# Attention output transposed and in column halves, scores in row halves, gate logits in strips of four tiles

## The chip, the cores and the metric

The kernel runs on one core of a Trainium2 chip. The metric is the device time of one execution in microseconds. TensorE (PE) multiplies matrices, VectorE (DVE), ScalarE (ACT) and GpSimd (POOL) work element by element, SyncE (SP) issues most DMAs. Every engine takes its instructions strictly in the order of the program and waits at an instruction until what it needs is there. TensorE works on operands in SBUF and writes into PSUM, which ACT and VectorE empty. Its clock is granted at one of two levels, 1.2 and 2.4 GHz.

## What is computed

Three stages follow one another. The attention is a recurrence with a decay per element, for 4 batches of 8 heads, 768 steps and head size 48:

```python
state = np.zeros((B, H, D, D), dtype=np.float32)
for t in range(S):
    state = alpha[:, :, t, :, None] * state + np.einsum('bhd,bhe->bhde', k[:, :, t], v[:, :, t])
    y[:, :, t] = np.einsum('bhd,bhde->bhe', q[:, :, t], state)
```

Its output, 3072 rows of 384, goes through a mixture of eight experts: `logits = x @ w_gate + modality_bias[modality_id]`, one expert per row (the argmax), `gate_w * (relu(x @ w1[e]) @ w2[e])` with the softmax weight of that expert. A dense layer follows, `relu(x @ w_in)**2 @ w_out`. All of it is in float32.

## The kernel before

The 3072 rows are 24 tiles of 128 (`NTILE`), six to a batch. The program is written out by hand in the order in which each engine is to run it; no scheduler changes it. The loop over the tiles (lines 732 to 776) does this in iteration n:

- TensorE: `kv_mm(n)`, the tile's contribution to the state; `qk_mm(n + 1)`, the scores of the next tile; `k_T(n + 1)`, its keys transposed (kp); `gate_T(n - 1)`, the output rows of the tile before, transposed for the gate; `y_mm(n)`; `gate_L(n - 1)`, its logits.
- VectorE: the state's update (st, sd) in `kv_mm`, then `prep(n + 3)`: the running products of the decay (acum), the reverse ones (rs), and queries and keys scaled by them (qt, kt). Behind these, weight conversions for the dense layer (`conv_v`, in iterations up to 15), the gate (`gate_a` and what follows), and from iteration 20 the splitting of expert weights (`pop`).
- ACT empties PSUM: scores (pa), kp (kT), the gate's transposes (xt), the output (xb); it builds two block-diagonal operands by copies, qbd of the queries (`q_bd`) and sbd of the state (`s_bd`); and it scales output rows by their gate weight (`scale`).
- GpSimd masks the scores (pm) and does a part of the conversions.

Heads stand in pairs: qt, kt and the state hold head 2p in partitions 0 to 47 and head 2p+1 in 64 to 111 (`RP` = 112). Before, a pair's scores are one matmul over 112 partitions with the block-diagonal qbd (256 columns), and y has the tile's rows in its partitions. `y_mm` first adds the part of the state (L514, from the second tile of a batch on), then that of the tile (L517). A float32 matmul leaves two records of the multiplication and two of the weight load in the trace (a transpose leaves one of each).

The tiles are gated in groups of 8, 8, 5 and 3 (`GROUPS`). Once a group's last tile is there, `gate_a` on VectorE finds the expert; in the next iteration `gate_b` on TensorE counts rows per expert and stands ahead of `y_mm`. After group 1 (tiles 8 to 15) the fullest expert is chosen, its weights are loaded, and rows for it are gathered (iteration 21), so that its matmuls (`mm1(0, f)`) start right behind the loop. `scale` and `store` write the scaled rows to DRAM (xs), from where the experts gather them. `ps_x` is a PSUM pool with one bank (tag "x"), which gate transposes, the row lists and the experts' transposes share. `open_moe` behind the loop lets GpSimd fill x2T with zeros, in the space that the attention leaves. Groups' functions and the loop, as the change touches them:

## Time and profile before

| | |
|---|---|
| runs | 870.28, 874.29, 2774.08 us (median 874.29) |
| profiled execution | 871.33 us, span 869.5 us |
| TensorE busy | 819.9 us (94%), weight loads 733.8 us (84%) |
| VectorE, ACT, GpSimd busy | 508.3 us (58%), 369.4 us (42%), 198.9 us (23%) |
| mean granted TensorE clock | 0.951 |

The attention takes the first quarter of the span: y of the last tile begins at 206.8 us. The experts' and the dense layer's matmuls fill the rest. A busy share is an average over the span; which engine sets the pace of a stage is read from the stage. Names such as `y<-vv,pm` say what an instruction writes and from what; L517 is a line of the kernel before.

### The profile page before, as it was taken

What the parts mean: (1) busy time and instruction counts of PE and PEld (TensorE: products, weight loads), DVE (VectorE), ACT (ScalarE), POOL (GpSimd) and SP (SyncE); (2) the same over time, 40 slices, a digit from 0 to 9 for tenths busy, and PEclk for the clock granted to TensorE, in tenths of its full rate; (3) what the DMA queues carried; (4) which work ended last, traced back from release to release, by engine and by line L of the source; (5) the groups of instructions that cost most, each with busy time, mean ns of one, the idle gap of its engine ahead of it and who ended that gap; (6) DMA issues with size and microseconds to landing.
All of it is one profiled execution on the core that took longest, in us unless ns stands there. A gap on an engine that the chain in (4) does not pass through costs nothing.

```text
span 869.5 us, 12270 instructions
## 1 busy us (share of the span) xinstructions
PE 819.9 (94%) x4704; PEld 733.8 (84%) x4704; DVE 508.3 (58%) x823; ACT 369.4 (42%) x663; POOL 198.9 (23%) x179
## 2 busy tenths in 40 slices
PE   6998789799889999999979999999999999999995
PEld 5988779699888778787868999999999999999985
DVE  7999999886747365464576444454454334334340
ACT  3655476296244344444445333333233234234331
POOL 6355355234123242331230001001001001000101
PEclk8888689699999999999989999999999999999998
DMA  9765475462445667558565002102100000000001
GB/s 238 188 195 178 145 249 163 135 196 96 137 118 185 179 127 203 113 185 157 86 217 145 21 1 83 51 1 77 58 1 28 11 0 23 15 1 19 19 0 41
DMA packets 42542, 88.75 MB, mean 102 GB/s; under 512 B 11134, under 2 KB 26522, under 8 KB 42474
## 3 DMA queue, kind: packets, MB, share of 16 engines
q1 hardware_dynamic: 39274, 78.04, 33.0%
q0 software_dynamic: 3200, 9.83, 3.5%
q8 instruction: 39, 0.64, 0.3%
q14 instruction: 29, 0.24, 0.1%
HBM read 72.10 MB, written 15.76 MB: 101 GB/s over the span
## 4 chain that ended last, share of the span: by engine, by line
PE 72%; DVE 18%; DMA 5%; ACT 2%; issue 2%; POOL 0%; SPq 0%; POOLq 0%; DVEq 0%; ACTq 0%
PE h L620 8%; PE h L621 8%; PE acc L621 8%; PE acc L619 8%; PE acc L620 8%; PE h L619 8%; PE oo L620 3%; PE hps L619 3%; PE hps L620 3%; PE oo L621 3%; PE oo L619 3%; PE hps L621 3%; DVE acum L435 3%; DVE rs L439 2%; PE y L517 2%
## 5 line engine op out<-in xcount | busy, mean ns | idle before, releaser
L966 DVE TENSOR_TENSOR r<-r 128x512 f32<-128x512 f32 x96 | 66.6, 693 | 149.5 <-ACT r L965 149.4
L621 PE MATMUL acc<-w2h,hl 128*128 128x384 f32 x376 | 126.8, 337 | 0.0
L965 ACT ACTIVATE r<-h 128x512 f32<-128x512 f32 x96 | 57.4, 598 | 162.9 <-PE h L621 161.0
L619 PE MATMUL acc<-w2h,hh 128*128 128x384 f32 x376 | 126.6, 337 | 0.0
L620 PE MATMUL acc<-w2l,hh 128*128 128x384 f32 x376 | 126.3, 336 | 0.0
L621 PE MATMUL h<-xh,w1l 128*128 128x512 f32 x288 | 113.9, 395 | 0.0
L620 PE MATMUL h<-xl,w1h 128*128 128x512 f32 x288 | 113.6, 395 | 0.0
L619 PE MATMUL h<-xh,w1h 128*128 128x512 f32 x288 | 112.2, 390 | 0.0
L989 POOL DMA_INDIRECT out_dram<-ob,pidx x24 | 24.3, 1011 | 383.9 <-ACT ob L987 346.5
L530 DVE TENSOR_TENSOR hl<-r,hh 128x512 fp32r<-128x512 f32 x94 | 65.1, 693 | 64.5 <-PE acc L621 39.8
L529 ACT CAST hh<-r 128x512 fp32r<-128x512 f32 x94 | 58.3, 621 | 75.5 <-DVE r L966 75.5
L620 PE MATMUL oo<-hl,w2h 128*128 128x512 f32 (+1 forms) x192 | 68.8, 358 | 6.4 <-DVE hl L881 6.4
L619 PEld LDWEIGHTS acc<-w2h,hh 128*128 128x128 f32 x376 | 70.7, 188 | 4.1
L620 PEld LDWEIGHTS acc<-w2l,hh 128*128 128x128 f32 x376 | 70.6, 188 | 4.0
L621 PEld LDWEIGHTS acc<-w2h,hl 128*128 128x128 f32 x376 | 70.5, 188 | 0.0
L881 DVE SCALAR_TENSOR_TENSOR hl<-hps,hh 128x512 fp32r<-128x512 f32 (+1 forms) x48 | 30.9, 644 | 67.5 <-ACT hh L880 67.5
L619 PE MATMUL hps<-xh,w1h 128*128 128x512 f32 (+1 forms) x192 | 67.8, 353 | 2.6 <-DVE hl L645 2.6
L619 PE MATMUL oo<-hh,w2h 128*128 128x512 f32 (+1 forms) x192 | 70.1, 365 | 0.0
L621 PE MATMUL oo<-hh,w2l 128*128 128x512 f32 (+1 forms) x192 | 68.5, 357 | 0.0
L465 POOL TENSOR_SCALAR_AFFINE_SELECT pm<-pa 128x512 f32<-128x512 f32 x48 | 49.4, 1039 | 82.8 <-ACT pa L463 82.5
L620 PE MATMUL hps<-xl,w1h 128*128 128x512 f32 (+1 forms) x192 | 67.2, 350 | 0.1
L621 PE MATMUL hps<-xh,w1l 128*128 128x512 f32 (+1 forms) x192 | 67.1, 349 | 0.0
(223 smaller groups left out, 1571.7 us busy)
## 6 DMA issues: line engine op xcount, KB each, us to landing
qk<-qka_dram SPq DMA_DIRECT2D x23, 675.5 KB, 5.3
raw<-w_dram SPq DMA_DIRECT2D x21, 512.0 KB, 7.9
raw<-w_dram SPq DMA_DIRECT2D x28, 384.0 KB, 3.6
raw<-w_in_dram SPq DMA_DIRECT2D x12, 512.0 KB, 6.2
cvr<-w_out_dram SPq DMA_DIRECT2D x12, 512.0 KB, 9.8
vv<-v_dram SPq DMA_DIRECT2D x24, 192.0 KB, 5.3
xs<-xb SPq DMA_DIRECT2D x24, 192.0 KB, 2.3
alr<-alpha_dram SPq DMA_DIRECT2D x9, 512.0 KB, 3.6
```

Of the source, the lines that this page charges most:

```text
L435: V.tensor_tensor_scan(acum.rearrange("p a c -> p (a c)"), al, one0.rearrange("p a c -> p (a c)"), 0.0, op0=ALU.mult, op1=ALU.max)
L439: V.tensor_tensor_scan(rs.rearrange("p a c -> p (a c)")[:, ::-1], al[:, ::-1], rz.rearrange("p a c -> p (a c)")[:, ::-1], 0.0, op0=ALU.mul ...
L465: G.affine_select(out=pmt, in_=pa, pattern=[[0, 4], [1, C]], compare_op=ALU.is_ge, fill=0.0, base=0, channel_multiplier=-1)
L529: A.copy(hi, raw)
L530: V.tensor_sub(lo, raw, hi)
L619: PE.matmul(o, ah, bh, start=start, stop=False)
L620: PE.matmul(o, ah, bl, start=False, stop=False)
L621: PE.matmul(o, al, bh, start=False, stop=stop)
L881: V.scalar_tensor_tensor(hl, o, 0.0, hh, op0=ALU.max, op1=ALU.subtract)
L965: A.activation(r, o, AF.Relu)
L966: V.tensor_mul(r, r, r)
L989: G.indirect_dma_start(out=out, out_offset=bass.IndirectOffsetOnAxis(ap=pidx[:, n:n + 1], axis=0), in_=ob, in_offset=None)
```

## The change

Scores: no block-diagonal queries any more. Each head's scores are a matmul of its own over its 48 partitions, heads of partitions 0 to 47 into one PSUM bank and those of 64 to 111 into another, in turns. Output: y is computed transposed, [112 partitions, 4 pairs, 128 rows]; the state's operand sbd becomes a 112 x 112 block matrix that is now the stationary one, and the tile's part is one matmul per head with v as stationary operand, into partitions 0 to 63 or 64 to 111 (the 16 columns over 48 are other data that nothing reads). Gate: the transposed output needs no transpose for the logits; `gate_lg` computes those of up to four tiles in four strips of 32 partitions, ACT copies them, and one transpose turns them back. `scale` now transposes the tile's output back to rows (four transposes into ps_x) and ACT scales while it empties PSUM, in two instructions; `store` follows at once. Up to three tiles an iteration are scaled, at three places (`ts`), where before three or four were scaled at its end.

```diff
@@ -116,21 +116,22 @@
...
-    NQ, NR = 2, 2
+    NR = 2
     one0 = at1.tile([RP, NP, CA], F32, name="one0")
     G.memset(one0, AMIN)
     G.memset(one0[:, :, :1], 1.0)
-    qbd = [at1.tile([RP, NP, 2, C], F32, name=f"qbd{i}") for i in range(NQ)]
-    sbd = [at1.tile([RP, NP, 2, D], F32, name=f"sbd{i}") for i in range(2)]
+    sbd = [at1.tile([RP, NP, RP], F32, name=f"sbd{i}") for i in range(2)]
     raz = [at1.tile([RP, NP, CA], F32, name=f"raz{i}") for i in range(NR)]
     for i in range(WARM):
         wps = ps_a.tile([128, 4, C], F32, tag="sp", name="warm", bufs=2)
         PE.matmul(wps.rearrange("p a c -> p (a c)")[:, :256], one0[:, 0, :128], one0.rearrange("p a c -> p (a c)")[:, :256], start=True, stop=True)
-    for t in raz + qbd + sbd:
+    for t in raz + sbd:
         G.memset(t, 0.0)
 
-    wg_sb = gc.tile([128, KD, NE], F32, name="wg_sb")
-    SY.dma_start(wg_sb, wg.rearrange("(k p) e -> p k e", p=128))
+    wg_sb = gc.tile([RP, NP, 32], F32, name="wg_sb")
+    G.memset(wg_sb, 0.0)
+    for j in range(2):
+        SY.dma_start(wg_sb[64 * j:64 * j + D, :, :NE], wg.rearrange("(p j d) e -> j d p e", j=2, d=D)[j])
...
@@ -196,27 +197,26 @@
 
     gst = {}
 
-    def gate_T(x):
-        xt_ps = ps_x.tile([128, 512], F32, tag="x", name="xt_ps")
-        for k in range(KD):
-            PE.transpose(xt_ps[:, k * 128:(k + 1) * 128], x[:, k * 128:(k + 1) * 128], ident)
-        xt = gt.tile([128, DM], F32, tag="xt", name="xt")
-        A.copy(xt, xt_ps[:, :DM])
-        return xt
-
-    def gate_L(g, i, xt):
-        if i == 0:
-            gst[g] = dict(lg=ps_g.tile([128, GM, NE], F32, tag="lg", name="lg"))
-        lg = gst[g]["lg"]
-        for k in range(KD):
-            PE.matmul(lg[:, i, :], xt[:, k * 128:(k + 1) * 128], wg_sb[:, k, :], start=(k == 0), stop=(k == KD - 1))
+    def gate_lg(g, i0, i1):
+        t0 = GROUPS[g][0]
+        lt = ps_g.tile([128, 128], F32, tag="lt", name="lt")
+        for p in range(NP):
+            for i in range(i0, i1):
+                q = slice(32 * (i - i0), 32 * (i - i0 + 1))
+                PE.matmul(lt[q, :], wg_sb[:, p, :], yts[t0 + i][:, p, :], start=(p == 0), stop=(p == NP - 1))
+        n = 32 * (i1 - i0)
+        ls = gt.tile([128, 128], F32, tag="ls", name="ls")
+        A.copy(ls[:n], lt[:n])
+        if i0 == 0:
+            gst[g] = dict(lg=ps_g.tile([128, GM, 32], F32, tag="rk", name="lg"))
+        PE.transpose(gst[g]["lg"][:, i0:i1, :].rearrange("p t e -> p (t e)"), ls[:n], ident[:n, :n])
 
...
-        V.tensor_add(L, lg[:, :T, :], lbias[:, t0:t0 + T, :])
+        V.tensor_add(L, lg[:, :T, :NE], lbias[:, t0:t0 + T, :])
...
@@ -268,10 +268,18 @@
 
     def scale(t):
         g, i = tile_group[t]
-        A.activation(xts[t], xts[t], AF.Copy, scale=gst[g]["gw"][:, i:i + 1])
+        xp_ = ps_x.tile([128, 512], F32, tag="x", name="xtr")
+        yt = yts.pop(t)
+        for p in range(NP):
+            PE.transpose(xp_[:, p * RP:(p + 1) * RP], yt[:, p, :], ident[:RP, :RP])
+        x = gt.tile([128, DM], F32, tag="xb", name="xb", bufs=3)
+        xv = xp_[:, :NP * RP].rearrange("s (p r) -> s p r", r=RP)
+        for j in range(2):
+            A.activation(x.rearrange("s (p j d) -> s j p d", j=2, d=D)[:, j], xv[:, :, 64 * j:64 * j + D], AF.Copy, scale=gst[g]["gw"][:, i:i + 1])
+        xts[t] = x
 
     def store(t):
-        SY.dma_start(xs[t * 128:(t + 1) * 128, :], xts[t])
+        SY.dma_start(xs[t * 128:(t + 1) * 128, :], xts.pop(t))
 
     def gate_bt(t):
         g, i = tile_group[t]
@@ -444,21 +452,17 @@
         ae = acum[:, :, C:C + 1]
         return dict(ae=ae, qt=qt, kt=kt)
 
-    def q_bd(n):
-        qb, qt = qbd[n % NQ], preps[n]["qt"]
-        A.copy(qb[0:D, :, 0, :], qt[0:D])
-        A.copy(qb[64:64 + D, :, 1, :], qt[64:64 + D])
-        preps[n]["qb"] = qb
-
-    preps, pms, kTs, sds, bds, xts, xtr = {}, {}, {}, {}, {}, {}, {}
+    preps, pms, kTs, sds, bds, xts, yts = {}, {}, {}, {}, {}, {}, {}
 
     def qk_mm(n):
         pr = preps[n]
         pm = []
-        for g in range(2):
-            sp = ps_a.tile([128, 4, C], F32, tag="sp", name="sp", bufs=2)
-            for p in range(2):
-                PE.matmul(sp[:, 2 * p:2 * p + 2, :], pr["kt"][:, 2 * g + p, :], pr["qb"][:, 2 * g + p], start=True, stop=True)
+        sps = [ps_a.tile([128, 4, C], F32, tag="sp", name="sp", bufs=2) for _ in range(2)]
+        for p in range(NP):
+            for j, sp in enumerate(sps):
+                rows = slice(64 * j, 64 * j + D)
+                PE.matmul(sp[:, p, :], pr["kt"][rows, p, :], pr["qt"][rows, p, :], start=True, stop=True)
+        for sp in sps:
             pa = at2.tile([128, 4, C], F32, tag="pa", name="pa")
             A.copy(pa, sp)
             pmt = at2.tile([128, 4, C], F32, tag="pm", name="pm", bufs=4)
@@ -501,24 +505,25 @@
         if n % NCH == 0:
             return
         bd, sd = sbd[n % 2], sds[n]
-        A.copy(bd[0:D, :, 0, :], sd[0:D])
-        A.copy(bd[64:64 + D, :, 1, :], sd[64:64 + D])
+        A.copy(bd[0:D, :, 0:D], sd[0:D])
+        A.copy(bd[64:64 + D, :, 64:64 + D], sd[64:64 + D])
         bds[n] = bd
 
     def y_mm(n):
         vv, pm, pr = vs.pop(n), pms.pop(n), preps[n]
-        y = ps_a.tile([128, H, D], F32, tag="y", name="y")
-        first = True
-        if n % NCH:
+        y = ps_a.tile([RP, NP, C], F32, tag="y", name="y")
+        cross = n % NCH > 0
+        if cross:
             for p in range(NP):
-                PE.matmul(y[:, 2 * p:2 * p + 2, :], pr["qt"][:, p, :], bds[n][:, p], start=first, stop=False)
-                first = False
-        for h in range(H):
-            PE.matmul(y[:, h, :], pm[h // 4][:, h % 4, :], vv[:, h, :], start=first, stop=(h == H - 1))
-            first = False
-        x = gt.tile([128, DM], F32, tag="xb", name="xb", bufs=12)
-        A.copy(x, y.rearrange("p h d -> p (h d)"))
-        xts[n] = x
+                PE.matmul(y[:, p, :], bds[n][:, p, :], pr["qt"][:, p, :], start=(p == 0), stop=False)
+        for p in range(NP):
+            for j in range(2):
+                w = 64 if j == 0 else D
+                vj = vv.rearrange("s h d -> s (h d)")[:, (2 * p + j) * D:(2 * p + j) * D + w]
+                PE.matmul(y[64 * j:64 * j + w, p, :], vj, pm[j][:, p, :], start=(p == 0 and not cross), stop=(p == NP - 1))
+        x = gt.tile([RP, NP, C], F32, tag="yt", name="yt", bufs=12)
+        A.copy(x, y)
+        yts[n] = x
 
...
@@ -703,12 +708,10 @@
             SY.dma_start(dst, cvr.pop(i))
 
     preps[0] = prep(0)
-    q_bd(0)
     qk_mm(0)
     k_T(0)
     loaded[3] = load(3)
     preps[1] = prep(1)
-    q_bd(1)
     setup_gate()
     preps[2] = prep(2)
     todo = {}
@@ -722,6 +725,14 @@
 
     N = NTILE
     early = []
+    todo_ts = []
+
+    def ts():
+        if todo_ts:
+            t = todo_ts.pop(0)
+            scale(t)
+            store(t)
+
...
@@ -740,13 +751,11 @@
             qk_mm(n + 1)
             k_T(n + 1)
         do(n, "pool")
-        if n > 0:
-            xtr[n - 1] = gate_T(xts[n - 1])
-        if n + 2 < N:
-            q_bd(n + 2)
+        ts()
         if n + 3 < N:
             preps[n + 3] = prep(n + 3)
         do(n, "mid")
+        ts()
         if n > GROUPS[EG + 1][0] + 3:
             pop(2)
         if n == N - 1:
@@ -755,10 +764,12 @@
         y_mm(n)
         if n + 1 < N:
             s_bd(n + 1)
+        ts()
         if n > 0:
             g, i = tile_group[n - 1]
-            gate_L(g, i, xtr.pop(n - 1))
             t0, T = GROUPS[g]
+            if i % 4 == 3 or i == T - 1:
+                gate_lg(g, i // 4 * 4, i + 1)
             if i == T - 1:
                 gate_a(g)
                 at(n + 1, "mid", lambda g=g: (gate_b(g), gate_s(g)))
@@ -771,13 +782,13 @@
                 d = 4 if g == EG else 3
                 for k in range(T):
                     at(n + 1 + k // 3, "end", lambda t=t0 + k: gate_bt(t))
-                    at(n + 2 + k // d, "end", lambda t=t0 + k: scale(t))
-                    at(n + 3 + k // d, "mid", lambda t=t0 + k: store(t))
+                    at(n + 2 + k // d, "pre", lambda t=t0 + k: todo_ts.append(t))
         do(n, "end")
-    xtr[N - 1] = gate_T(xts[N - 1])
     for n in range(N, N + 4):
         for k in ("pre", "pool", "mid", "end"):
             do(n, k)
+        while todo_ts:
+            ts()
     drain(("w2", 0))
     actx.close()
     open_moe()
@@ -785,11 +796,11 @@
     t0, T = GROUPS[-1]
     mm1(0, 0)
     mm1(0, 1)
-    g, i = tile_group[N - 1]
-    gate_L(g, i, xtr[N - 1])
+    g = len(GROUPS) - 1
+    gate_lg(g, 0, T)
+    mm1(0, 2)
     gate_a(g)
     gate_s(g)
-    mm1(0, 2)
     mm1(0, 3)
     gate_b(g)
     gate_c(g)
```

On TensorE, from the scores in iteration 20 on (sp scores, kp keys transposed, xt_ps transposes for the gate, y output, lg and lt logits, xtr transposes back, kv the state). Before:

```order
L461 MATMUL sp<-qbd_122,kt 128x256 x4
L474 MATMUL kp<-ident,kt 128x112 x4
L202 MATMUL xt_ps<-ident,xb 128x128 x3
L514 MATMUL y<-sbd_125,qt 128x96 x4
L517 MATMUL y<-vv,pm 128x48 x8
L212 MATMUL lg<-wg_sb,xt 128x8 x3
L488 MATMUL kv<-vv,kT 64x48
```

Now:

```order
L464 MATMUL sp<-qt,kt 128x128 x8
L478 MATMUL kp<-ident,kt 128x112 x4
L274 MATMUL xtr<-ident,yt 128x112 x8
L518 MATMUL y<-qt,sbd_122 112x128 x4
L523 MATMUL y<-pm,vv 64x128
L523 MATMUL y<-pm,vv 48x128
...
L206 MATMUL lt<-yt,wg_sb 32x128 x16
L212 MATMUL lg<-ident,ls 128x128
L492 MATMUL kv<-vv,kT 64x48
```

The transposes of two tiles stand ahead of y; the logits of four tiles and their transpose stand ahead of the next kv.

On ACT, from the output's copy in iteration 19 on (yt and xb the output, sbd the state's operand, pa scores, kT keys). Before:

```order
L520 COPY xb<-y 128x384
L504 COPY sbd_125<-sd 48x4x48
L505 COPY sbd_125<-sd 48x4x48
L271 ACTIVATE xb<-xb,gw 128x384 x4
L463 COPY pa<-sp 128x512 x2
L476 COPY kT<-kp 128x448
L204 COPY xt<-xt_ps 128x384
L449 COPY qbd_123<-qt 48x4x128
L450 COPY qbd_123<-qt 48x4x128
```

Now:

```order
L525 COPY yt<-y 112x512
L508 COPY sbd_122<-sd 48x4x48
L509 COPY sbd_122<-sd 48x4x48
L278 ACTIVATE xb<-xtr,gw 128x4x48 x2
L467 COPY pa<-sp 128x512 x2
L480 COPY kT<-kp 128x448
L278 ACTIVATE xb<-xtr,gw 128x4x48 x4
L534 CAST w1h_169<-raw 128x1024 x2
L525 COPY yt<-y 112x512
```

The scalings of two tiles stand behind pa and kT, and read what TensorE has just transposed.

On TensorE, from y of the last tile to the first expert matmuls (hps). Before:

```order
L514 MATMUL y<-sbd_125,qt 128x96 x4
L517 MATMUL y<-vv,pm 128x48 x8
L212 MATMUL lg<-wg_sb,xt 128x8 x3
L202 MATMUL xt_ps<-ident,xb 128x128 x3
L619 MATMUL hps<-xh,w1h_171 128x256
```

Now:

```order
L518 MATMUL y<-qt,sbd_123 112x128 x4
L523 MATMUL y<-pm,vv 64x128
L523 MATMUL y<-pm,vv 48x128
...
L274 MATMUL xtr<-ident,yt 128x112 x12
L624 MATMUL hps<-xh,w1h_169 128x256
```

Three tiles' transposes back stand between them; three more follow between the fourth and the fifth column block of the first expert.

## Rows read from the trace of the kernel before

**Rows 1.** Windows by stage: busy us (count) of PE, PEld, DVE, ACT, POOL; clock, DMA.
```profile
33.00:163.00 130.00, 111.80 (x865) 103.08 (x864) 125.56 (x189) 76.92 (x155) 67.12 (x56) 0.85 0.59 175
163.00:190.00 27.00, 27.00 (x212) 25.44 (x210) 23.52 (x49) 16.34 (x34) 6.28 (x6) 0.79 0.64 200
190.00:212.00 22.00, 21.05 (x193) 20.11 (x193) 14.87 (x40) 16.63 (x33) 6.31 (x7) 0.92 0.27 75
250.00:869.50 619.50, 600.73 (x2993) 531.14 (x2993) 292.23 (x415) 231.38 (x385) 88.95 (x67) 0.99 0.28 74
```

**Rows 2.** Waits of DVE, 24 to 212 us: total us, times, longest us.
```profile
DVE w1l L530 <- ACT w1h L529: 3.6, 1, 3.6
DVE st L494 <- PE kv L488: 2.2, 4, 1.0
DVE sd L497 <- PE kv L488: 1.6, 1, 1.6
```

**Rows 3.** Waits of PE, 24 to 212 us.
```profile
PE rk L235 <- DVE oh_all L228: 10.3, 3, 5.5
```

**Rows 4.** Timeline, 150 to 190 us: start, us, engine, line; half clock up to 174.2.
```profile
163.19 2.00 PE L514 MATMUL y<-sbd,qt 112*128 112x96 f32 x8
164.98 3.54 PE L517 MATMUL y<-vv,pm 128*128 128x48 f32 x16
169.66 1.09 PE L488 MATMUL kv<-vv,kT 128*64 128x48 f32 x16
170.68 3.70 PE L461 MATMUL sp<-qbd,kt 112*128 112x256 f32 x8
...
174.61 0.49 PE L202 MATMUL xt_ps<-ident,xb 128*128 128x128 f32 x3
174.94 1.88 PE L517 MATMUL y<-vv,pm 128*128 128x48 f32 x16
176.66 0.80 PE L212 MATMUL lg<-wg_sb,xt 128*128 128x8 f32 x6
177.39 0.67 PE L488 MATMUL kv<-vv,kT 128*64 128x48 f32 x16
...
179.81 0.55 PE L474 MATMUL kp<-ident,kt 112*128 112x112 f32 x4
...
183.87 0.67 PE L488 MATMUL kv<-vv,kT 128*64 128x48 f32 x16
```

**Rows 5.** Timeline, 100 to 135 us, full clock: kv, scores and weight loads.
```profile
114.82 0.54 PEld L488 LDWEIGHTS kv<-vv,kT 128*64 128x64 f32 x16
114.82 0.67 PE L488 MATMUL kv<-vv,kT 128*64 128x48 f32 x16
115.41 1.99 PE L461 MATMUL sp<-qbd,kt 112*128 112x256 f32 x8
...
117.85 1.86 PEld L517 LDWEIGHTS y<-vv,pm 128*128 128x128 f32 x16
```

**Rows 6.** Windows by granted clock (third figure from the end).
```profile
160.50:174.20 13.70, 11.35 (x63) 10.48 (x63) 11.56 (x31) 2.56 (x5) 0.70 (x1) 0.50 0.49 131
204.90:208.30 3.40, 3.40 (x18) 3.40 (x17) 2.63 (x10) 2.56 (x6) 0.00 (x0) 0.50 0.00 0
```

**Rows 7.** ACT's groups, 0 to 215 us: busy us, mean ns; idle before, releaser.
```profile
L463 ACT COPY pa<-sp 128x512 f32<-128x512 f32 x48 | 27.5, 585 | 32.2 <-PE sp L461 29.7 <-POOL edesc_i L145 2.2
...
L504 ACT COPY sbd<-sd 48x192 f32<-48x192 f32 x20 | 7.0, 351 | 15.8 <-DVE sd L495 12.3 <-DVE sd L497 3.4
```

**Rows 8.** Line L441 (qt) on DVE: ns, least, median, most.
```profile
L441 DVE TENSOR_TENSOR qt<-qk,acum x24: 659/1051/1458, 6.5 to 188.1; 112x512 f32<-112x512 f32 x24
```

**Rows 9.** Timeline, 210 to 220.5 us.
```profile
210.42 9.07 POOL L630 MEMSET x2T<- 128x10752 f32 x1 [8.39 <-PE y L517]
...
216.09 3.42 DVE L264 TENSOR_SCALAR ss<-ss 128x3 f32<-128x3 f32 x1
```

**Rows 10.** Waits of PE, 212 to 250 us.
```profile
PE hps L619 <- DVE hl L645: 2.6, 2, 2.4
```

## The prediction

> **What bounds the kernel now.** I read the windows by stage first [rows 1]. From 33 to 163 us VectorE is busy 125.6 of 130 us (97%) and TensorE 111.8. From 163 to 190 TensorE is busy for all 27 us, from 190 to 212 for 21.05 of 22, and from 250 to the end for 600.7 of 619.5. So the page's "PE 94%" is an average over stages with different limits: in the first two thirds of the attention VectorE sets the pace, in its last third TensorE does, and after 250 us only the expert matmuls count, which the change leaves alone.
>
> Next the waits. In 24 to 212 us VectorE waits for TensorE five times, 2.2 + 1.6 = 3.8 us in all; its only long wait is 3.6 us for ACT's cast of w1 [rows 2]. In the same stretch TensorE waits 10.3 us, in three waits, for the one-hot of the gate, the longest 5.5 us [rows 3]. So where VectorE is the limit, a faster TensorE only waits longer.
>
> Then the timeline of one tile, at both clocks [rows 4, 5]. At full clock a tile costs TensorE kv 0.67, scores 1.99, kp 0.55, gate transposes 0.49, the state's part of y 1.0 (half of 2.00 at half clock), y 1.88 and logits 0.80: 7.4 us of durations. At half clock they nearly double (scores 3.70, y 3.54, kv 1.09). The clock windows [rows 6] show the half level after a wait (160.5 to 174.2) and once without one: 204.9 to 208.3, with TensorE busy all 3.4 us on transposes and part of y.
>
> **The change, part by part.** The sum is made against the profiled execution, 871.33 us (span 869.5); the median of the three runs is 874.29, so that execution is 3 us below it.
>
> *TensorE's price per tile at full clock.* Scores: 16 records of 128 columns instead of 8 of 256; if the two row halves overlap, half of 1.99 = 1.0, if not, still 1.99. The state's part: the same 8 records, 128 columns wide, where each loaded 128 before: 1.0. y: 16 records of 128 columns on 64 or 48 output rows. Before, each loaded 128 columns in 1.86/16 = 0.116 us [rows 5]; now each streams 128. Do column halves overlap? The kv matmuls are such halves already: their 16 loads of 64 and 48 columns would take 8 x 0.058 + 8 x 0.044 = 0.82 us in a row, and took 0.54 [rows 5]. So they do, and y is half of 1.88 = 0.94. Logits: 32 records per four tiles in four strips, 8 x 0.116 = 0.93, or 0.23 a tile. Transposes back: four, as kp, 0.55. Sum 0.67 + 1.0 + 0.55 + 1.0 + 0.94 + 0.23 + 0.55 = 4.9, so 2.5 us less per tile, 60 us of TensorE time over 24. ACT loses both qbd copies and the xt copy, and gets two scalings of 192 elements for one (0.35 each by the sbd row [rows 7]); it is busy 76.9 of 130 us and sets no pace.
>
> *Up to 163 us: nothing.* VectorE's instructions are the same, and it is busy 97%. What hides ACT and TensorE here is VectorE's own 8.5 us an iteration (130 us over some 15). The cover lasts: the new waits (TensorE's transposes of logits wait for ACT's copy of the strips, which stands behind sbd, which waits for VectorE's sd) end some 1.5 us after sd, and kv of the next tile is wanted a whole VectorE iteration later. One bound: GpSimd's masks may fall elsewhere. qt takes 0.66 us at least and 1.05 at the median [rows 8]; all 24 moved in or out is 24 x 0.39 = 9 us, either way. I take 0: in most iterations ACT's pa stands behind sbd and so behind sd, in both kernels, which pins the masks.
>
> *163 to 190 us (iterations 17 to 20): -1.7.* The 3.8 us of waiting for kv, 1.0 of them already at 24 us, can go. What is late next is ACT. scale() now begins with transposes into the one bank of ps_x, and each iteration issues three; the second must wait for the first one's scaling, which on ACT stands behind pa, pa and kT: 3 x 0.585 (kT is a little shorter) + 0.7 = 2.4 us after the scores, where TensorE has only kp and the first transposes, 1.1, to do. Behind it in TensorE's queue stand y, the third transposes and kv. The path of an iteration is kv 0.67 + scores 1.0 + 2.4 + 0.55 + y 1.94 + 0.55 = 7.1 us, against 6.5 before (kv to kv, 177.39 to 183.87 [rows 4]). Three iterations (18 to 20) scale, so 3 x 0.7 = 2.1 is given back: -3.8 + 2.1. The stores sit behind the scalings on SP and can delay a load there by about one scaling, 0.7; loads run three tiles ahead, so nothing.
>
> *190 to 212 us: +0.8.* VectorE's 3.6 us wait for w1 goes (xt and qbd no longer stand before the cast on ACT). Late next: the logits of tiles 16 to 19, then of tile 20: gate matmuls 0.93, ACT's yt 0.59 (as pa), sbd 2 x 0.35 and strips 0.3, then a transpose, all ahead of kv in TensorE's queue, and at tile 19 two casts of w1 stand before them on ACT. I price that at 2 us of the 3.6: -1.5. After y of the last tile three transposes-and-scalings follow one another before the first expert matmul, about 1.2 us each (0.55 + 0.7), 3.6 in the place of the logits and transposes of before (0.80 + 0.49): +2.3.
>
> *212 to 250 us: +0.3.* The last gate's strips: +0.5. GpSimd's memset of x2T (9.07 us) ends at 219.49, where VectorE's 3.42 us "ss" ends too [rows 9], and TensorE's wait of 2.4 [rows 10] follows from that. The memset waits for y of the last tile, which comes 1.5 earlier: -1.5. Three more scalings, 3.7 us, now stand between the fourth and fifth expert matmul where those 2.4 were idle: +1.3.
>
> After 250: 0. Sum: 0 - 1.7 + 0.8 + 0.3 = -0.6, so 870.7: **871 us**, with 865 to 876 for this case.
>
> **The rivals.**
> *Row halves don't overlap* (the change doesn't do what it says): for column halves a row speaks, for row halves none. Scores stay at 1.99; in the six iterations where TensorE or its path counts, 6 x 1.0 = +6: **877**. The Trainium skill, "TensorEngine Tiling (Array Packing)", section Key Properties, says that different tiles load and multiply in parallel, and that a change of tiling mode drains TensorE. Overlapping column halves agree with the first; no row here shows row halves. By the second the five changes per tile would come on top; the nearest one in this trace, from kv's halves to the scores, shows kv ending at 115.49 (114.82 + 0.67) and scores starting at 115.41, no gap.
>
> *TensorE stays at half clock* (the slow side): from iteration 18 to the last tile. Where it scales, the path is kv 1.09 + scores 1.85 + ACT 2.4 + transposes 1.1 + y 2.0 + 1.77 + transposes 1.1 = 11.3 for 6.5, +4.8 x 3 = 14; in the last three iterations kv 1.09 + scores 1.85 + kp 1.1 + y 3.8 + logits 1.9 = 9.7 for 7.3 (22 us over three [rows 1]), +2.4 x 3 = 7; less the 1.7: **891**, slower by 2%. It decides where the granted clock of 163 to 212 stays under about 0.6. For it: TensorE gets idler, gets waits of 1 to 2 us and more transposes, and 204.9 to 208.3 fell to half with no wait. Against it: at half clock it is busy without a break, and 11.4 us of that brought the full level back at 174.2 [rows 6]. The Trainium skill, "TensorE: Matmul & The Clock Gate", Part 4, says that transposes do not count as activity like matmuls do. The stretch at 204.9 fits that; by it this case gets likelier, as four transposes a tile replace three and stand alone between waits.
>
> *TensorE is the bound and the saving arrives:* ACT's waits hide. Then iterations 18 to 20 fall to VectorE's 5.9 (23.5 us over four [rows 1]; -0.4 each, without the waits), 21 to 23 from 7.3 to 5.3 (-2 each), and the waits for kv go, 3.8: -11, **860**. For it: 27 of 27 us busy. Against: the ACT chain above is made of rows. With all masks off qt as well, 851.
>
> **How the numbers follow.** Forecast 0.52, row halves serial 0.18, half clock 0.13, saving arrives 0.14, the latter with moved masks 0.03. The time is the likeliest case's, 871. The range 860 to 886 leaves out the half clock case but for its mild end, and half of the fast one. Measurement tells 2% (17 us) from no change. Below 857: the last case and the edge of the fast one, 0.05. Above 892: the upper half of the half clock case and both slow cases together, 0.08. Within: 0.87.
>
> **What the profile after would show.** VectorE at 95% or more from 33 to about 163, and the gate's one-hot done near 162: right for "nothing". Scores' 16 records in about 1.0 us at full clock: row halves overlap; 2.0: they don't. y's 16 in about 0.95. TensorE waiting for ACT's scaling before the second transposes, 1 to 2 us, in iterations 10 to 12 and 18 to 20. The first expert matmul at 210 to 212. The forecast is wrong if VectorE's own time up to 163 moves by over 5 us, or if it waits for kv longer than 3.8 us in all.

## The result, and the profile after

| | median us | runs |
|---|---|---|
| before | 871.31 | 868.88 to 2774.08, 14 runs |
| changed | 879.54 | 875.30 to 883.04, 14 runs |

The changed kernel takes 1.0097 of the time of the one before, 95% interval 1.0083 to 1.0111: about 8 us more. That is within 2% and within the range, but it is a loss that can be told apart from nothing, where a gain of 0.6 us was forecast. The profiled execution took 882.66 us (span 880.9), 3 us above its median, and that of before 871.33, at its median. One run of the kernel before (2774.08 us), and two runs each of rows and rowsd below, the profiled one of rowsd among them, which took about 2% longer than the fastest of their kernel, are left out of the ratios.

The windows by stage, as in [rows 1], with the last two cut at 212 and 250 us:

```profile
33.00:163.00 130.00, 92.19 (x968) 79.60 (x967) 125.56 (x189) 51.48 (x113) 58.39 (x53) 0.72 0.58 175
163.00:190.00 27.00, 18.65 (x210) 16.09 (x209) 22.19 (x52) 13.94 (x33) 7.09 (x6) 0.82 0.53 175
190.00:212.00 22.00, 18.03 (x239) 15.12 (x238) 13.69 (x35) 15.04 (x33) 5.67 (x7) 0.92 0.32 100
212.00:250.00 38.00, 33.83 (x295) 32.03 (x296) 26.14 (x84) 10.54 (x30) 9.91 (x3) 0.87 0.28 95
250.00:880.90 630.90, 609.55 (x3047) 539.09 (x3045) 298.27 (x432) 235.46 (x392) 94.23 (x71) 0.99 0.28 75
```

Up to 163 us VectorE is busy 125.56 us, to the hundredth what it was, while TensorE falls from 111.8 to 92.2 and ACT from 76.9 to 51.5. So 20 and 25 us of busy time are saved there and nothing comes of it, as forecast. Of the matmuls (timeline; start, duration, engine, line), at half clock first:

```profile
145.47 2.08 PE L464 MATMUL sp<-qt,kt 48*128 48x128 f32 x16
149.45 1.97 PE L523 MATMUL y<-pm,vv 128*64 128x128 f32 x16
...
170.50 1.09 PE L523 MATMUL y<-pm,vv 128*64 128x128 f32 x16
172.05 0.67 PE L492 MATMUL kv<-vv,kT 128*64 128x48 f32 x16
172.65 1.16 PE L464 MATMUL sp<-qt,kt 48*128 48x128 f32 x16
```

Scores take 1.16 us for 1.99 [rows 5] and y 1.09 for 1.88 [rows 4]: row halves and column halves both overlap, and from kv to the scores there is again no gap (172.05 + 0.67 is past 172.65).

The first loss is in iteration 20 (timeline; behind a row the idle time before it and what ended it):

```profile
175.65 1.42 SPq L545 DMA_DIRECT2D raw<-w_dram  x3
177.26 0.39 SPq L556 DMA_DIRECT2D raw<-w_dram  x1
177.75 3.17 SPq L282 DMA_DIRECT2D xs<-xb  x3
...
186.57 0.73 ACT L278 ACTIVATE xb<-xtr,gw 128x192 f32<-128x192 f32 x2 [4.17 <-DMA xs<-xb]
...
187.36 1.01 PE L274 MATMUL xtr<-ident,yt 112*128 112x112 f32 x4 [5.63 <-ACT xb L278]
...
190.00 1.97 PE L523 MATMUL y<-pm,vv 128*64 128x128 f32 x16
...
190.15 1.22 DVE L535 TENSOR_TENSOR w1l<-raw,w1h 128x1024 fp32r<-128x1024 f32 x1 [4.03 <-ACT w1h L534]
```

`xb` now has three buffers. The scaling at 186.57 writes the one whose store was issued three tiles earlier, behind four weight loads of 384 to 512 KB, and waits 4.17 us for it to land. In the DMA issues from 174 to 190 us (count, KB each, median us to landing) such a store takes 8.7; from 160 to 195 us the least is 1.8:

```profile
xs<-xb SPq DMA_DIRECT2D x5, 192.0 KB, 8.7
...
DMA to landing us min/median/max: 1.8/1.9/8.7
```

Behind this scaling wait TensorE's transposes (5.63 us), y, and ACT's cast of w1, so the very wait of VectorE for w1 that the change was to remove is back with 4.03 us [rows 2].

The second loss is the tail:

```profile
210.95 9.06 POOL L635 MEMSET x2T<- 128x10752 f32 x1 [6.08 <-issue]
...
211.60 8.56 DVE L286 TENSOR_SCALAR bt_all<-rev,lof,tokid 128x128 f16<-128x128 f32 x2
...
212.18 0.60 PE L274 MATMUL xtr<-ident,yt 112*128 112x112 f32 x4 [0.82 <-ACT xb L278]
...
213.65 0.71 PE L274 MATMUL xtr<-ident,yt 112*128 112x112 f32 x4 [0.87 <-ACT xb L278]
214.05 0.56 PE L624 MATMUL hps<-xh,w1h 128*128 128x256 f32 x1
...
224.38 1.01 PE L274 MATMUL xtr<-ident,yt 112*128 112x112 f32 x4 [0.87 <-ACT xb L278]
226.26 1.01 PE L274 MATMUL xtr<-ident,yt 112*128 112x112 f32 x4 [0.87 <-ACT xb L278]
...
233.15 0.75 PE L314 MATMUL idpe<-e_aeb,bt_all 128*128 128x2 f16 x24
```

Two of these rows in the kernel before, the first expert matmul (hps) and idpe:

```profile
211.18 0.36 PE L619 MATMUL hps<-xh,w1h 128*128 128x256 f32 x1
...
223.89 0.76 PE L306 MATMUL idpe<-e_aeb,bt_all 128*128 128x2 f16 x24
```

TensorE and ACT take turns over the one bank of `ps_x`. The first expert matmul starts at 214.05 (211.18 before), and the granted clock falls twice around these transposes (windows; clock third from the end):

```profile
214.00:217.40 3.40, 3.40 (x19) 3.40 (x18) 3.40 (x2) 1.11 (x3) 3.40 (x1) 0.50 0.31 116
224.20:231.10 6.90, 5.85 (x27) 5.50 (x28) 2.62 (x11) 1.97 (x6) 0.00 (x0) 0.51 0.26 89
```

The row that all kernels below are compared by is **idpe**, the 24 matmuls that end the plan of the last group. They start 9.3 us later than before, and in every profile below the span ends 644 to 649 us after them (before: 869.5 - 223.9 = 645.6; changed: 647.8). So most of what an edit is worth shows in when idpe starts. A profile is one execution, though, up to 3 us off the median of its kernel, and that of the changed kernel is 3 us above: differences of 2 or 3 us between two profiles are no finding by themselves. `bt_all`, which the plan needs, is a table of row numbers that VectorE writes tile by tile.

### The profile page after: what moved, and what is told of

It is laid out like the page before. It is cut to its first block, busy times and chain, and to the rows that moved or that the text cites. A ratio compares the mean times of both kernels' runs of the same rounds, so it can differ in the third digit from the quotient of the medians.

```text
span 880.9 us, 12761 instructions
## 1 busy us (share of the span) xinstructions
PE 794.6 (90%) x4975; PEld 701.1 (80%) x4975; DVE 512.5 (58%) x823; ACT 338.5 (38%) x622; POOL 194.6 (22%) x178
## 4 chain that ended last, share of the span: by engine, by line
PE 67%; DMA 3%; DVE 2%; ACT 1%; issue 1%; POOL 0%; POOLq 0%; DVEq 0%; SPq 0%
PE h L625 8%; PE h L626 8%; PE acc L626 8%; PE acc L624 8%; PE h L624 7%; PE acc L625 7%; PE hps L625 3%; PE hps L626 3%; PE hps L624 3%; PE oo L625 3%; PE oo L626 3%; PE oo L624 3%; DMA cvr<-w_out_dram 2%; DMA xg<-xs,ids 1%; PE xt L617 1%; DVE xl L535 1%
```

## The experiments

All ratios are to the kernel before, run beside on the same chip.

| kernel | ratio, 95% interval | idpe starts, us |
|---|---|---|
| changed | 1.0097, 1.0083 to 1.0111 | 233.15 |
| xb5: five buffers | 1.0015, 0.9997 to 1.0033 | 226.07 |
| tail: scalings spread | 1.0030, 1.0014 to 1.0046 | 226.41 |
| both | 0.9978, 0.9955 to 1.0002 | 222.85 |
| lsfirst: strips early | 1.0054, 1.0035 to 1.0073 | 228.99 |
| all: these three | 0.9968, 0.9954 to 0.9983 | 219.18 |
| bothv: both, memset on VectorE | 1.0052, 1.0033 to 1.0071 | 226.17 |
| bothp: both, memset in pieces | 0.9972, 0.9953 to 0.9990 | 219.22 |
| allp: all, memset in pieces | 0.9954, 0.9935 to 0.9973 | 218.29 |
| afterp: changed, memset in pieces | 1.0114, 1.0081 to 1.0146 | 231.99 |
| beforep: before, memset in pieces | 0.9931, 0.9905 to 0.9957 | 220.66 |
| sfull: changed, scores as before | 1.0103, 1.0075 to 1.0131 | 229.67 |
| rows: before, row halves alone | 1.0216, 1.0171 to 1.0260 | 238.93 |
| rowsd: rows, one matmul more a tile | 1.0215, 1.0185 to 1.0245 | - |
| rowseq: rows, four and four | 1.0801, 1.0768 to 1.0834 | 292.60 |

**xb5.**

```diff
-        x = gt.tile([128, DM], F32, tag="xb", name="xb", bufs=3)
+        x = gt.tile([128, DM], F32, tag="xb", name="xb", bufs=5)
```

> The changed kernel with five buffers xb for the scaled rows in the place of three; nothing else. Theory: in iteration 20 the first scaling waits 4.17 us until the store of three tiles earlier has landed behind the weight loads, and TensorE behind it 5.63 us. With five buffers it waits for a store issued before those loads: that wait of ACT is under 0.5 us, TensorE's falls to the 1.4 us of iterations 18 and 19, y of tile 20 starts at about 186 (190.0 with three buffers), and 3 to 6 us of the 8.2 come back: about +2 to +5 us against the kernel before (ratio 1.002 to 1.006). Rival (the half clock costs the time, or the drains of mode changes): the waits for stores are a symptom; ratio stays at 1.009 to 1.011. Rival (they come back but the tail, which has the same limit, takes them): y of tile 20 early, but the first expert matmul still at 213 to 214.

Measured 1.0015: 7 of the 8 us come back, a little more than the theory's 3 to 6. In iteration 20 ACT waits for no store, and TensorE for what it waits in the two iterations before, 1.36 us:

```profile
182.38 0.60 PE L274 MATMUL xtr<-ident,yt 112*128 112x112 f32 x4 [1.36 <-ACT xb L278]
...
183.78 1.09 PE L523 MATMUL y<-pm,vv 128*64 128x128 f32 x16
...
226.07 0.75 PE L314 MATMUL idpe<-e_aeb,bt_all 128*128 128x2 f16 x24
```

y of tile 20 starts at 183.8 (190.0), and the 7 us stay: the first expert matmul starts at 206.9 (214.05), and idpe too is 7.1 us earlier. VectorE's wait for w1 falls to 1.6 us (4.03). Both rivals fall.

**tail.** (`...` stands for lines left out.)

```diff
-        ts()
+        if n < N - 1:
+            ts()
...
-        while todo_ts:
-            ts()
...
     mm1(0, 0)
+    ts()
     mm1(0, 1)
+    ts()
...
     mm1(0, 2)
+    ts()
...
     for t in range(t0, N):
-        scale(t)
-        store(t)
         gate_bt(t)
+    scale(t0)
+    store(t0)
     mm1(0, 4)
...
+    scale(t0 + 1)
+    store(t0 + 1)
     mm1(0, 5)
+    scale(t0 + 2)
+    store(t0 + 2)
```

> The changed kernel with the six last scalings spread out: those of tiles 18 to 20 one behind each of the first three expert matmul groups, in the place of all ahead of the first; those of tiles 21 to 23 behind the gate's plan, and one behind each of the expert matmul groups 3, 4 and 5. Nothing is left out. Theory: the back-to-back transposes and scalings through one bank, and the half clock after them, cost 6 to 8 us; the first expert matmul starts at 211 to 212 (214.0), there is no half clock from 214 to 235, the gather's transposes start at 252 to 255 (259.95), and the time is about +1 to +4 us against the kernel before (ratio 1.001 to 1.005). Rival (the gather starts late because the last plan on VectorE and the stores are late, whatever TensorE does): the same waits appear at the gather; ratio 1.008 to 1.011.

Measured 1.0030, 5.8 us back, as the theory has it. The first expert matmul starts at 208.9, earlier than foreseen; but 2.3 us of what its profile is ahead stand in front of the edit (y of tile 20 at 187.75 for 190.00) and belong to the execution, so the medians are the better measure. One thing was not as expected: TensorE now waits 2.78 us for hl, the low part of the expert's activations that VectorE splits off, and matmuls at half clock follow:

```profile
218.08 0.57 PE L624 MATMUL hps<-xh,w1h 128*128 128x256 f32 x1 [2.78 <-DVE hl L650]
...
220.33 0.99 PE L274 MATMUL xtr<-ident,yt 112*128 112x112 f32 x4
```

**both.**

> Five buffers xb and the six last scalings spread out, together. Theory: both parts come back, and what is left is the 4 us that the attention gained: -2 to -6 us against the kernel before (ratio 0.993 to 0.998). Rival (one of them is the cover of the other): no better than the better of the two alone, ratio 1.001 or more.

Measured 0.9978: 10.4 us below the changed kernel, where the two alone give 7.1 and 5.8; the interval just reaches 1. They do share a cover. VectorE is held for 8.5 us beside GpSimd's memset. In the changed kernel the scalings hide that (afterp below); here TensorE waits 2.78 us for hl behind it:

```profile
203.75 9.07 POOL L635 MEMSET x2T<- 128x10752 f32 x1 [6.09 <-issue]
204.39 8.56 DVE L286 TENSOR_SCALAR bt_all<-rev,lof,tokid 128x128 f16<-128x128 f32 x2
```

**lsfirst.**

```diff
-        if n + 1 < N:
-            s_bd(n + 1)
-        ts()
         if n > 0:
...
                 gate_lg(g, i // 4 * 4, i + 1)
+        if n + 1 < N:
+            s_bd(n + 1)
+        ts()
+        if n > 0:
```

> The changed kernel with the strips of logits (and ACT's copy of them) ahead of the copies sbd of the next tile and of the third scaling, in the place of behind them; nothing else. Theory: TensorE's waits of 3 to 5 us for this copy lie beside VectorE's work, so they shrink (15.7 us in five to under 8) and the time stays within 1.5 us of the changed kernel (ratio 1.008 to 1.0115). Rival (these waits, or the half clock that follows them, are what costs): 4 to 8 us come back, ratio 1.000 to 1.005.

Measured 1.0054, 3.7 us back: outside my 1.5 us and just short of the rival's 4. The waits shrink as foreseen (PE's waits from 24 to 215 us: total, times, longest; 15.7 in five before the edit):

```profile
PE lg L212 <- ACT ls L209: 2.3, 6, 0.4
```

Up to tile 20 nothing is gained. y of tile 23 comes 1.2 us earlier (208.5 for 209.7), and from 191.6 to 256.4 us the clock does not fall (1.00 in that window), so that from the first expert matmul to idpe 16.2 us pass for 19.1. The two add up to the 4.2 us by which idpe is earlier. Why the clock holds in this one and not in the changed kernel, with the same transposes, is open.

**all.**

> Five buffers xb, the six last scalings spread out, and the strips of logits ahead of sbd and of the third scaling. Theory now, after the strips alone gave 3.2 us: about 1 us comes from the waits for ls at tiles 21 to 23, which no VectorE work covers, and the rest was the half clock of the tail, which spreading the scalings has taken away already: 0.5 to 2 us below the kernel with the first two, ratio 0.995 to 0.9975. Rival (the strips are worth their whole 3 us wherever the scalings stand): ratio 0.993 to 0.9945.

Measured 0.9968, in the theory's range, and the interval begins above the rival's range (0.9945). But that is only 1 us below the kernel with both, and the two intervals overlap: that the strips give anything on top is not shown.

**bothv and bothp.**

```diff
-        G.memset(pools["x2T"], 0.0)
+        V.memset(pools["x2T"], 0.0)
```

```diff
-        G.memset(pools["x2T"], 0.0)
+        for k in range(KD):
+            for c in range(0, NT + PAD, 512):
+                G.memset(pools["x2T"][:, k, c:c + 512], 0.0)
```

> Five buffers and spread scalings, and the memset of x2T on VectorE in the place of GpSimd. Theory: in the kernel with both, VectorE's bt_all stands for 8.5 us beside GpSimd's memset of 9.07 us, so the gate of the last group starts 4.5 us late and TensorE waits 2.8 us for hl; with the memset on VectorE that block is gone, and if the memset takes under 5 us there, ids_b comes 3 to 4.5 us earlier and the time is 1.5 to 4.5 us lower (ratio 0.993 to 0.996); if it takes 9 us, nothing changes. Rival (bt_all is slow for another reason, such as the loads): bt_all still takes over 4 us.

> Five buffers and spread scalings, and GpSimd's memset of x2T in 21 pieces of 512 columns in the place of one of 10752. Theory (VectorE's instruction waits for a whole instruction of GpSimd): bt_all waits for one piece, 0.43 us, at most two, and ends by 206; the gain is that of the row above, 1.5 to 4.5 us (ratio 0.993 to 0.996). Rival (GpSimd keeps what they share through a row of instructions): bt_all ends at about 213 as before, and the ratio stays at 0.997 to 0.999.

On VectorE the memset takes 9.02 us, and the kernel is slower, 1.0052: the case "if it takes 9 us", and worse than "nothing changes", as VectorE now does it ahead of the split that TensorE waits for (5.5 us for hl). With pieces VectorE's bt_all takes its usual time:

```profile
205.24 0.59 DVE L286 TENSOR_SCALAR bt_all<-rev,lof,tokid 128x128 f16<-128x128 f32 x2
205.69 10.00 POOL L637 MEMSET x2T<- 128x512 f32 x21 [7.60 <-issue]
```

idpe is 3.6 us earlier than in the profile of the kernel with both, but the median ratio, 0.9972, is not told apart from 0.9978 and lies in the rival's range, though bt_all ends by 206 as the theory says. Nor does this profile show the pieces at work, as bt_all started just ahead of the first. So it did in the kernel with all three edits and a whole memset (203.94 for 204.82), while in the kernel with both it came 0.64 us behind it and was held for 8.5. Which of them comes first turns on about a microsecond; how often each outcome comes in a series of runs was not counted.

**beforep and afterp**, the same pieces in the two kernels.

> The kernel before with GpSimd's memset of x2T in 21 pieces; nothing else. Theory: VectorE's ss takes 0.2 us in the place of 3.42, and TensorE's wait of 2.4 us for hl goes: 1 to 2.5 us lower, ratio 0.997 to 0.999. Rival (the gather that follows is waited for anyway, or the pieces hold VectorE as long in sum): ratio 0.9995 or more. What the change is worth with all edits is read against this kernel.

> The changed kernel with GpSimd's memset of x2T in 21 pieces of 512 columns; nothing else. Theory (the block is part of the loss): bt_all takes 0.34 us for 8.5, TensorE's logits and hl of the first expert matmuls are not held, and 3 to 6 us come back as in the kernel before with pieces: ratio 1.003 to 1.006. Rival (the scalings hold the last gate just as long: its logits are there at 219.3 and VectorE comes free at 220.1): at most 1 us, ratio 1.0085 to 1.010.

beforep: 0.9931, 6 us, more than twice what was expected. The instruction that took 3.42 us in [rows 9] takes 0.49 with pieces running beside it:

```profile
209.63 10.21 POOL L632 MEMSET x2T<- 128x512 f32 x21 [8.39 <-PE y L517]
...
215.30 0.49 DVE L264 TENSOR_SCALAR ss<-ss 128x3 f32<-128x3 f32 x1
```

idpe starts at 220.66, 3.2 us earlier, of which 0.8 stand in front of the memset (the logits ahead of it at 209.36 for 210.14); the 2.4 that are left lie within what was expected. A span 1.8 us shorter behind idpe is all that the profile shows of the rest, and where the rest of the 6 us comes from is open. afterp: no gain (1.0114). Here the rival is right: with bt_all free, idpe moves by 1.2 us, and 1.1 of these stand in front of the edit (the transposes of iteration 20 at 186.27 for 187.36). The three scalings are in TensorE's way in both. VectorE's instruction there shows how a piece holds it, for part of a microsecond:

```profile
209.81 10.01 POOL L637 MEMSET x2T<- 128x512 f32 x21 [6.08 <-issue]
210.46 0.96 DVE L286 TENSOR_SCALAR bt_all<-rev,lof,tokid 128x128 f16<-128x128 f32 x2
```

The Trainium skill, "SBUF — State Buffer", section Who interferes with whom, says that a VectorE instruction in a two-port mode, which tensor_scalar can enter, and a GpSimd instruction shut each other out of the shared ports for a whole instruction. These rows agree: 8.56 and 3.42 us beside one long memset, each over as the memset ends (220.16 for 220.01, 219.51 for 219.49 [rows 9]), and at most 0.96 for two beside pieces of about half a microsecond. Kinds differ: a TENSOR_REDUCE on VectorE took its usual 0.17 us beside the memset of the kernel before (at 215.88).

**allp.**

> The best of the edits together: five buffers xb, spread scalings, strips ahead of sbd, and GpSimd's memset in 21 pieces. Theory: in the kernel without pieces VectorE's bt_all ended 0.3 us before the memset began, so the block was dodged by luck; the pieces take away the runs where it is not: 0 to 2 us lower, ratio 0.994 to 0.997. Rival (pieces change nothing): 0.9968 again; more pieces that hold VectorE more often: over 0.998.

Measured 0.9954: the best version of the change, 4 us below the kernel before, in the theory's range, though the interval holds the rival's 0.9968 too. But against the kernel before with the same pieces it is no gain (0.9931; medians of 866.9 and 864.6 us beside one another, intervals that overlap). Its first expert matmul starts 6 us earlier than there (204.4 for 210.4), and 14 us pass from it to idpe in the place of 10: the three scalings stand in that stretch. 2.4 us of lead are left at idpe, and at the end 0.5 of span.

**rows and rowsd.**

```diff
-            for p in range(2):
-                PE.matmul(sp[:, 2 * p:2 * p + 2, :], pr["kt"][:, 2 * g + p, :], pr["qb"][:, 2 * g + p], start=True, stop=True)
...
+            for j, sp in enumerate(sps):
+                rows = slice(64 * j, 64 * j + D)
+                PE.matmul(sp[:, p, :], pr["kt"][rows, p, :], pr["qt"][rows, p, :], start=True, stop=True)
...
```

rowsd has ahead of these

```diff
+        PE.matmul(sps[0], pr["kt"][:, 0, :], pr["qt"], start=True, stop=True)
```

> The kernel before with one part of the change alone: scores from row halves of qt, without the copies qbd; y, the gate and the scaling as before. Nothing is left out. Theory: the 16 records take about 1.1 us for 2.0, and ACT loses two copies per tile, but VectorE sets the pace up to 163 us; what can come is the 3.8 us of waits for kv and about 0.9 us in each of the last tiles, and nothing waits for it anew: -2 to -6 us (ratio 0.993 to 0.998). Rival (TensorE is the bound): 0.9 us of each of 24 tiles, -12 us or more (ratio under 0.987). Rival (the row halves, their mode changes or a colder TensorE cost the time): slower than the kernel before.

> The kernel with row-half scores alone, and one matmul of 128x512 more per tile ahead of them, over all rows, into a bank that the scores then write over: work that computes nothing that is used, about 1.0 us at full clock (half of the 1.99 us that eight records of 256 columns took). Theory: the kernel with row halves alone lost 21 us because TensorE, busy 134 of 139 us, was held at the lower clock for 78.5 us in a row; with the added matmul in each tile the granted clock from 24 to 163 us is back at 0.75 or more (0.60), and the time falls, to a ratio of 0.998 to 1.010. Rival (TensorE is simply too full, row halves cost something that the records don't show): with 1.0 us more per tile it gets slower still, by 10 us or more, ratio over 1.03.

Row halves alone cost 2.2%, the third case of their expectation. TensorE's window, 24 to 163 us (before: 120.80 busy at 0.84):

```profile
24.00:163.00 139.00, 134.32 (x994) 129.59 (x992) 125.01 (x189) 56.33 (x121) 67.76 (x54) 0.60 0.58 171
...
77.10:155.60 78.50, 75.02 (x478) 72.47 (x475) 68.80 (x112) 30.58 (x66) 34.76 (x27) 0.50 0.56 172
```

From 77.1 to 155.6 us the clock stays at the lower level. TensorE is busy 75.0 of these 78.5 us and VectorE only 68.8; a tile takes TensorE 10.8 us from scores to scores (129.28 to 140.09), without a gap. So TensorE becomes the bound, and VectorE waits for kv (9.4 us in four waits from 24 to 215 us).

rowsd does not settle why: neither back at 1.00 nor over 1.03, but the same 1.0215. Its profile is not read here. In the three runs behind its ratio the mean granted clock over the span was 0.925 to 0.939, against 0.891 to 0.898 in the runs of row halves alone and 0.950 to 0.958 in the kernel before. So the clock came back in part and the time did not. Either the added work takes what the clock gives, or the clock is not all that costs the 2.2%.

**sfull.**

```diff
...
-                PE.matmul(sp[:, p, :], pr["kt"][rows, p, :], pr["qt"][rows, p, :], start=True, stop=True)
...
+                PE.matmul(sp[:, 2 * p:2 * p + 2, :], pr["kt"][:, 2 * g + p, :], qbd[:, 2 * g + p], start=True, stop=True)
...
-        x = gt.tile([RP, NP, C], F32, tag="yt", name="yt", bufs=12)
+        x = gt.tile([RP, NP, C], F32, tag="yt", name="yt", bufs=11)
...
```

> The changed kernel with the scores as before: copies qbd (one buffer instead of two) and eight records of 256 columns; eleven buffers yt instead of twelve, for room. All else as changed. Theory (row halves are a gain within the change too, as TensorE's work is under VectorE's at either clock): from 163 us on it loses 0.9 us in each of the last tiles and ACT's copies return: 2 to 6 us above the changed kernel, ratio 1.012 to 1.017. Rival (row halves hold the clock down in the change as they do alone): the granted clock from 24 to 163 us rises from 0.73 to over 0.8, that of 163 to 260 to over 0.92, and the time falls by 2 to 6 us, ratio 1.003 to 1.0075.

The granted clock from 24 to 163 us does rise, from 0.73 to 0.84, as the rival says:

```profile
24.00:163.00 139.00, 101.59 (x983) 85.82 (x981) 134.18 (x203) 80.00 (x160) 64.54 (x58) 0.84 0.61 181
```

But the time stays (1.0103 against 1.0097): neither case. Within the change no run tells row halves from whole rows. Up to 163 us VectorE is busy 134.18 us of these 139 (134.22 with row halves) and covers TensorE at either clock. Behind that, longer scores and a higher clock (0.99 for 0.88 from 215 to 260 us) may cancel; that is not shown.

**rowseq.**

```diff
-        for p in range(NP):
-            for j, sp in enumerate(sps):
+        for j, sp in enumerate(sps):
+            for p in range(NP):
```

> Row-half scores alone, as before, but the four matmuls of the upper rows first and then the four of the lower, in the place of pairs; the same 16 records. Theory (what holds the clock down is that matmuls use fewer rows at a time): the records no longer overlap but for one pair, scores take 1.6 to 2.0 us at full clock for 1.16, TensorE stays as long or longer at the lower clock (granted 0.60 or less from 24 to 163 us), ratio 1.02 to 1.04. Rival (it is the alternation between row halves): the granted clock comes back to 0.75 or more, and the ratio to under 1.01.

The theory's direction, far past its size: 1.0801. TensorE is busy for all 139 us and never leaves half clock in that stretch:

```profile
24.00:163.00 139.00, 139.00 (x799) 134.83 (x799) 103.94 (x157) 49.93 (x101) 54.90 (x44) 0.50 0.49 148
```

The same 16 records take 3.09 us at that clock, in pairs (rows) 2.08:

```profile
135.18 3.09 PE L455 MATMUL sp<-qt,kt 48*128 48x128 f32 x16
...
140.09 2.08 PE L455 MATMUL sp<-qt,kt 48*128 48x128 f32 x16
```

The rival, that the alternation holds the clock down, falls.

## Why the prediction was wrong

- **Up to 163 us, nothing: right.** VectorE 125.56 us in both.
- **Both kinds of halves overlap: right**, 1.16 and 1.09 us for the 1.0 and 0.94 of the sum. The rival with serial row halves falls.
- **163 to 190 us, the 3.8 us of waits for kv: right.** The last `prep` starts 4.5 us earlier (its acum at 180.9 for 185.4). One wait of 2.6 us for kv is left, at 195.1, behind the store's wait.
- **The 2.1 us given back to ACT's scaling: the wait is there, its price is not.** TensorE waits 1.36 us before the second transposes in iterations 18 and 19, and from kv to kv 7.0 us pass (172.05 to 179.05), the 7.1 of the sum. But VectorE does not wait for it, as its own work covers it.
- **"The stores sit behind the scalings on SP ... so nothing": this step failed.** It asked whether a store could delay a load on SP, and never whether a load could delay a store, and the store the buffer that the next scaling writes. The diff shows `bufs=3` where there were 12. Giving it five takes back 7 us. The -1.5 us for w1 behind it turned into a wait of 4.0 through the same cause: with five buffers it is 1.6.
- **Three scalings after the last y, +2.3: right in size.** From the end of y to the first expert matmul 3.2 us pass (0.9 before).
- **212 to 250 us, +0.3: mis-sized.** From the first expert matmul to idpe 19.1 us pass for 12.7 before, +6.4. The second three scalings cost about what was summed; what was left out is the half clock around both triples, about 3 us by the kernel with early strips, where it does not fall and the same stretch takes 16.2.
- **The memset comes earlier and frees VectorE, -1.5: wrong.** It holds another instruction of VectorE for 8.5 us. In the changed kernel that is covered by the scalings; once they are spread it is not.
- **The rival "TensorE stays at half clock" had its place wrong.** From 163 to 212 us the granted clock was 0.82 and 0.92, not under 0.6. In the change the half clock costs most in the tail, as far as the runs show. With row halves alone, and y as long as before, TensorE is the bound while it lasts.
- **The range held by luck.** 879.5 lies in it through the store, which no case of the prediction priced, and a tail that was mis-sized, and near the 877 of a rival that falls. The chances also leave nothing for 857 to 860 and for 886 to 892: 0.05, 0.08 and 0.87 are all there is.

The losses overlap, so their single gains (7.1, 5.8 and 3.7 us) add up to more than the 11.2 that come back together. With all of them gone the change is ahead of the kernel before by 3 to 4 us, close to the 4.5 that the attention gained. That the kernel before reaches 864.6 us with the pieces alone, and so matches all of this, had not been foreseen, and its 6 us are explained only in part.

## What to carry to other kernels

When an edit moves a buffer from one use to another, follow the ring to its end: who frees it, through which transfer, and what is queued ahead of that transfer at that moment. When work of an off-path engine is bunched at the end of a stage, price the alternation through its one bank and the lower clock that follows, and look for work in which to spread it. And read one late landmark (here idpe) in every profile: where the rest of the span hardly changes, it tells most of what an edit is worth, to within the microseconds by which one execution differs from the median. What two profiles differ by in front of an edit is not the edit's.

## What the hardware showed unexpectedly

- The granted clock of TensorE does not follow from being busy alone. With scores over 48 rows at a time it was busy 139.00 of 139 us at 0.50; with scores over 112 rows 120.80 of 139 at 0.84. The Trainium skill, "TensorE: Matmul & The Clock Gate", section Why this matters for your kernels, advises to keep TensorE continuously busy for the most matmul throughput; in that stretch it did not do. Which property of the row halves counts is not settled: a matmul more over all rows raised the mean clock and did not bring the time back.
- Matmuls in two row halves run in pairs when the halves alternate (2.08 us at half clock) and partly when they come four and four (3.09), against 3.70 for the block-diagonal form [rows 4].
- A VectorE instruction on 128x3 elements took 3.42 us beside a memset of GpSimd, and cutting that memset into 21 pieces made the kernel before 0.7% faster, more than the profile accounts for.
